# Preparing the token columns of a channel loop in two halves, placed behind the casts of the states

## The chip, the cores and the metric

The kernel runs on one core of one Trainium2 chip. The metric is the device time of one execution in microseconds (us), as the median of several runs. Before the change it is 2973.82 us, the median of 3 runs that lie between 2972.2 and 2982.99 us.

## The reference, cut to what matters

The program is the forward pass and all gradients of a gated layer. One branch is attention with 32 heads over 2048 tokens of width 576. The other is a diagonal state-space layer: each of 576 channels has 128 complex states and is convolved with a kernel K built from them. A sigmoid gate mixes the two.

```python
P = jnp.exp(logdA[:, :, None] * l[None, None, :])        # 576 x 128 x 2048
K = jnp.einsum("dn,dnl,dn->dl", Cc, P, dB).real
y = irfft(rfft(u, 2L) * rfft(K, 2L))[:L] + u * Dskip     # causal convolution
g = sigmoid((x * gate_w).sum(-1, keepdims=True))
out = g * attention(x) + (1 - g) * y
```

(The second half of this fence is condensed.) The output and the gradients of x, the weights, the state-space parameters and the gate are wanted.

## The kernel before, in words

The program runs in stages: projections, then the long attention stage (forward and backward), then a **channel loop** for the state-space branch, then a final stage that makes the weight gradients. The change touches the channel loop only. On the clock of the profile the loop fills roughly 2200 to 2768 us.

The loop handles the 576 channels in 18 blocks of 32 (`CB = 32`, `NBLK = 18`); two blocks make a pair of 64 channels (`XB = 2 * CB`). Time is cut into 16 chunks of 128 tokens (`NB = 16`, `NS = 15` chunk borders). The helpers, with their lines:

- `load_rx` (L879 to L884) loads, for a pair, the token columns of the input (xr_d) and of the incoming gradient (gyr_d) into `RXn`. There is one buffer of it.
- `prep_rx` (L886 to L891) turns `RXn` into `RX`, with three instructions on ScalarE (ACT): a reordering copy (L889), and two products with a column of token numbers (L890, L891). `RX` has two buffers; a buffer holds a pair. `m_fin` (L933) later adds two more columns per channel.
- `turn_e` (L946) transposes a half block of the powers E on TensorE (PE) and copies the result out on ACT (`E1e`, L957).
- `uv` (L968) multiplies `E1e` by the columns of `RX` on PE and copies the product out on ACT (`UV`, L982).
- `scan` (L984) is the recurrence over the 15 chunk borders. It runs on VectorE (DVE): 14 steps of three dependent instructions (L995, L998, L999) that make `HG`, the states.
- `casts` (L1001) makes bfloat16 copies of the states on ACT: `hR` and `gR` (L1006) and `CK` (L1008).
- `rw1`, `rw2` (L1010 to L1021) make the weights `Rw` on DVE from `HG`.
- `t0`, `ybp` (L1038, L1047) accumulate the outputs in PSUM on PE from `RX`, `T0w` and `Rw`; ACT copies them out (`yd`, L1059).
- `pairs1`, `pairs2` (L1077, L1084) are products of `UV` with `hR` and `gR` on DVE (`pq`, L1065 and L1093), summed on PE.
- `m_part` (L902), `m_skw` (L920), `m_sum` (L928), `k0` (L1023) serve the block that comes later: matmuls on PE, copies on ACT (`mst` L912, `wk` L1027, `K0c` L1035), and a trip through memory.

Iteration i of the loop (L1134) works on several blocks at once: block i (scan, casts, outputs, products), block i+1 (`uv`, second half of `turn_e`, `k0`), block i+2 (`turn_e` first half, `m_sum`, `m_fin`) and block i+3 (loads, `m_part`). In the source, `sb` is i+2. The loop also has a first round with i = -1, which has no current block.

The order of the work on PE, ACT, DVE and GpSimd (POOL) is written out by hand: L873 switches the scheduler off for these four engines, so each runs its instructions in the order in which the loop calls them. The queue of the transfers (SP) isn't in that list; its order is worked out when the program is built. Each of the engines works through its own list in order and waits at the first instruction whose input or buffer isn't there.

So the place where the loop calls `prep_rx` decides what stands behind it on ACT. Before the change it is called every second iteration, when i+2 is even, for a whole pair, ahead of `scan` and `casts`. On ACT, which has no part in the scan, it therefore stands directly before the casts `hR` and `gR` of the current block.

Of the kernel before, what the change touches and what calls it, by code (L numbers as in the profile page):

```python
# [11 lines left out]
BF = mybir.dt.bfloat16  # L12
# [5 lines left out]
P = 128  # L18


def build(tc, aps, dbg_aps=None, stages=("s1", "attn", "post", "s4", "final")):
# [7 lines left out]
    def mm(out, lhsT, rhs, start=True, stop=True, **kw):  # L29
        return nc.tensor.matmul(out, lhsT=lhsT, rhs=rhs, start=start, stop=stop, **kw)  # L30
# [31 lines left out]
    with ExitStack() as gctx:  # L62
# [38 lines left out]
        CB = 32  # L101
# [327 lines left out]
        if "attn" in stages:  # L429
# [5 lines left out]
            with ExitStack() as ctx:  # L435
# [266 lines left out]
                for G in range(NTOT + OFF + 24):  # L702
# [4 lines left out]
                    if G < NTOT:  # L707
                        u, s = divmod(G, NST)
                        g, b = units[u]
# [11 lines left out]
                    if r1:  # L721
                        g, b, i, j0 = r1
# [14 lines left out]
                    elif 0 <= m_ < NTOT // 8:  # L737
                        u_, kq = divmod(m_, NQ)
                        g, b = units[u_]
# [12 lines left out]
                        else:  # L752
                            p = 2 * kq + (slot == 4)
# [5 lines left out]
                    if r2:  # L759
                        g, b, s2 = r2  # L760
# [16 lines left out]
                    if G % 8 in (0, 3, 4, 7) and G >= 3:  # L777
                        i_ = (G - 3) // 8 * 4 + {3: 0, 4: 1, 7: 2, 0: 3}[G % 8]
                        u_, i_ = divmod(i_, NT)
                        if 0 <= u_ < NU:  # L780
                            g, b = units[u_]
# [13 lines left out]
                    for (kind, g, b, i, j, ps) in rows:  # L795
# [9 lines left out]
                        else:  # L805
# [6 lines left out]
                            if U["dsn", i] == nj:  # L812
                                p = i // 2
# [14 lines left out]
        if "s4" in stages:  # L828
            XB = 2 * CB
# [10 lines left out]
            with ExitStack() as ctx:  # L840
                pc = ctx.enter_context(tc.tile_pool(name="s4l", bufs=1))
                pw = ctx.enter_context(tc.tile_pool(name="s4lw", bufs=1))
# [31 lines left out]
                NCOL = 64  # L874
                CU0, CV0, CU1, CV1, CDK = 0, NB, 2 * NB, 2 * NB + NS, 2 * NB + 2 * NS
                RXs, BK = {}, {}
                ydx = {}

                def load_rx(xb):  # L879
                    d0 = xb * XB  # L880
                    RXn = pw.tile([P, 2 * NB, XB], BF, tag="RXn", bufs=1, name="RXn")
                    nc.sync.dma_start(RXn[:, 0:NB, :], xr_d[:, :, d0:d0 + XB])
                    nc.sync.dma_start(RXn[:, NB:2 * NB, :], gyr_d[:, :, d0:d0 + XB])
                    RXs[xb] = [RXn, None]  # L884

                def prep_rx(xb):  # L886
                    RXn = RXs[xb][0].rearrange("p k c -> p c k")
                    RX = RXs[xb][1] = pw.tile([P, XB, NCOL], BF, tag="RX", bufs=2, name="RX")
                    nc.scalar.copy(RX[:, :, 0:2 * NB], RXn)  # L889
                    nc.scalar.mul(RX[:, :, CU1:CU1 + NS], RXn[:, :, CU0:CU0 + NS], l1col)  # L890
                    nc.scalar.mul(RX[:, :, CV1:CV1 + NS], RXn[:, :, CV0:CV0 + NS], l0col)  # L891

                xss = {}

                def m_load(b):
                    xs = xss[b] = pw.tile([P, NSUB, SUB, CB], BF, tag="xs", bufs=2, name="xs")
                    src = bass.AP(tensor=xb_d.tensor, offset=xb_d[b:b + 1, 0:1, 0:1].offset,
                                  ap=[[XR * SUB * CB, NB], [SUB * CB, NSUB], [1, NSUB * SUB * CB]])
                    nc.sync.dma_start(xs.rearrange("p e t c -> p (e t c)"), src)
                    nc.sync.dma_start(gyp2[b % 2][:, 0:SUB, :].rearrange("p t c -> p (t c)"), gyb_d[b])  # L900
# [14 lines left out]
                def dkp(b):  # L915
                    return misc2[(b + 1) % 2][:, 12 * CB:13 * CB]
# [3 lines left out]
                def m_skw(b):  # L920
                    skw = skws[b] = pw.tile([P, CB // 8, P], F32, tag="skw", name="skw")
                    for v in range(CB // 8):
                        dd = b * CB + v * 8
                        src = bass.AP(tensor=Md_d.tensor, offset=Md_d[dd:dd + 1, 0:1, SUB - 1:SUB].offset,
                                      ap=[[2 * SUB * MW, 8], [MW - 1, SUB], [1, P]])
                        nc.sync.dma_start(skw[:, v, :], src)
# [6 lines left out]
                def m_fin(b):  # L933
                    RX = RXs[b // 2][1]
                    o = (b % 2) * CB
                    pk = dkp(b)
                    nc.scalar.copy(RX[:, o:o + CB, CDK], pk)
                    nc.scalar.mul(RX[:, o:o + CB, CDK + 1], pk, l0col)
                    nc.scalar.copy(dDs_row[:, b * CB:(b + 1) * CB], pk[0:1, :])

                def blk(b):
                    if b not in BK:
                        B_ = BK[b] = dict(E={}, En={})
                    return BK[b]
# [14 lines left out]
                def load_par(b):  # L959
                    par = blk(b)["par"] = pw.tile([P, 12, CB], F32, tag="par", bufs=2, name="par")  # L960
                    nc.sync.dma_start(par, par_d[:, 0:12, b * CB:(b + 1) * CB])

                def load_en(b, h):
                    dG = b * CB + h * GS
                    En = blk(b)["En"][h] = pw.tile([P, GS, 2, P], BF, tag="E1n", bufs=6, name="E1n")
                    nc.sync.dma_start(En, E_d[:, dG:dG + GS])

                def uv(b, h):  # L968
                    B_ = blk(b)
                    if h == 0:  # L970
                        B_["UV"] = pw.tile([P, 2, NCOL, CB], BF, tag="UV", bufs=2, name="UV")
                    UV = B_["UV"]
                    E_ = B_["E"].pop(h)
                    RX = RXs[b // 2][1]
                    off = (b % 2) * CB + h * GS
                    for q in range(2):
                        for ri in range(2):
                            pr = pps.tile([P, NCOL, 8], F32, tag="bk", bufs=4, name="uvp")
                            for c_ in range(8):
                                mm(pr[:, :, c_], lhsT=E_[:, q * 8 + c_, ri, :], rhs=RX[:, off + q * 8 + c_, :])  # L980
                            c0 = h * GS + q * 8
                            nc.scalar.mul(UV[:, ri, :, c0:c0 + 8], pr, -1.0 if ri == 0 else 1.0)  # L982
# [40 lines left out]
                def k0(b):  # L1023

                    B_ = blk(b)
                    wk = pw.tile([P, 2, CB], BF, tag="wk", bufs=2, name="wk")
                    nc.scalar.copy(wk, B_["par"][:, 10:12, :])  # L1027
                    kps = misc2[b % 2][:, 13 * CB:14 * CB]
                    mm(kps, lhsT=ident_bf[0:1, :], rhs=dsk_row[:, b * CB:(b + 1) * CB], start=True, stop=False)
                    for ch in range(CB):  # L1030
                        for ri in range(2):
                            mm(kps[:, ch:ch + 1], lhsT=B_["En"][ch // GS][:, ch % GS, ri, :], rhs=wk[:, ri, ch:ch + 1],
                               start=False, stop=(ch == CB - 1 and ri == 1))
                    K0c = pw.tile([P, CB], BF, tag="K0c", bufs=2, name="K0c")
                    nc.scalar.copy(K0c, kps)  # L1035
                    nc.sync.dma_start(Kp_d[b, P:2 * P, :], K0c)
# [97 lines left out]
                for i in range(-1, NBLK):  # L1134
                    cur = i >= 0
                    nx = i + 1 < NBLK
                    mb = i + 3 if i + 3 < NBLK else None
                    sb = i + 2 if i + 2 < NBLK else None
                    if sb is not None:
                        m_skw(sb)  # L1140
                    if sb is not None:
                        load_par(sb)
                    if mb is not None:
                        m_load(mb)
                    if sb is not None and sb % 2 == 0:
                        load_rx(sb // 2)
                    if nx and cur:
                        k0(i + 1)
                    if nx:
                        uv(i + 1, 0)  # L1150
                        turn_e(i + 1, 1, 0, 4)
                    if sb is not None and sb % 2 == 0:
                        prep_rx(sb // 2)
                    if cur:
                        scan(i, 0, 15)
                        casts(i)
                        rw1(i)
                        rw2(i)
                        t0(i, 0)
                        t0(i, 1)  # L1160
                    if nx:
                        uv(i + 1, 1)
                    if cur:
                        if nx:
                            t0_load(i + 1)
                        ybp(i, 0)
                        ybp(i, 1)
                        pairs1(i)
                    if cur and mb is not None:
                        load_en(mb, 0)  # L1170
                        load_en(mb, 1)
                    if sb is not None:
                        turn_e(sb, 0, 0, 4)
                        m_sum(sb)
                        m_fin(sb)
                    if cur:
                        pairs2(i)
                        sums(i)
                    if mb is not None:
                        m_part(mb, 0)  # L1180
                        m_part(mb, 1)
                    if cur:
                        BK.pop(i)
# [256 lines left out]
```

## Time and profile before

| | |
|---|---|
| time, median of 3 | 2973.82 us |
| span of the profiled execution | 2976.5 us |
| PE, DVE, ACT, POOL busy over the span | 83%, 79%, 80%, 54% |
| channel loop, 2262 to 2768 us: DVE, PE, ACT busy | 434.85, 386.21, 341.98 us of 506 |
| DMA engines busy in the same stretch, mean | 69% |
| reordering copy L889, 9 times, median | 3820 ns |
| products L890 and L891, 9 times each, medians | 2039 and 2104 ns |

How to read it: the shares over the whole span mix stages with different limits. The table's lower half is for the channel loop. DVE is the busiest engine there, and still not always busy; the question in this loop is what each engine waits for, and in which iterations. The views used are the timeline of each engine (a row is a run of like instructions with its start, its time from first start to last end, the count, and in brackets the idle time just before it with what ended it), the sums of waits, and the busy time by stretches.

### The profile page before, as it was taken

Reading aid. Unit: us, or ns where it says so; the run is one execution under the profiler, and the core shown is the slowest. Engines: PE = TensorE matmul, PEld = TensorE weight load, DVE = VectorE, ACT = ScalarE, POOL = GpSimd, SP = SyncE. Lnnn points to the kernel's source line nnn. Section 1 sums busy time; section 2 is a strip of 40 time slices with the busy share of each in tenths; the row PEclk is TensorE's granted clock in tenths of the full one; section 3 lists DMA queues with packets and bytes.
Section 4 is the critical chain, followed back from the end, with each engine's and each line's share of the span. In section 5 each row is a group of like instructions: output and inputs, shape, how many; then the busy total and the mean of one; then the engine's idle time right before and its main releaser. Section 6 shows DMA issues by size and latency. Waiting matters only on the chain.

```text
span 2976.5 us, 69573 instructions
## 1 busy us (share of the span) xinstructions
PE 2468.2 (83%) x27132; PEld 1186.9 (40%) x27132; DVE 2359.4 (79%) x4147; ACT 2373.2 (80%) x2765; POOL 1605.9 (54%) x2653
## 2 busy tenths in 40 slices
PE   4768988998988888889898889898847887876779
PEld 2432333332333233233333233333226777776457
DVE  4435998997998889799899889989937888889634
ACT  2449999999999999899999999999736777675111
POOL 1038888888887788778888878878010000000010
PEclk8877999998999999899999999999968888887889
DMA  8855999989989989998988998998788877872886
GB/s 224 160 152 107 159 155 169 163 158 165 171 147 165 167 155 167 160 157 155 168 165 154 164 161 153 166 165 153 130 196 217 209 201 208 206 194 66 244 211 132
DMA packets 1293343, 499.99 MB, mean 168 GB/s; under 512 B 1187774, under 2 KB 1263136, under 8 KB 1283796
## 3 DMA queue, kind: packets, MB, share of 16 engines
q1 hardware_dynamic: 1264500, 434.91, 77.2%
q0 software_dynamic: 20624, 53.26, 7.3%
q10 hardware_dynamic: 7888, 7.38, 0.8%
q8 instruction: 212, 3.47, 0.5%
q14 instruction: 119, 0.97, 0.1%
HBM read 144.48 MB, written 99.69 MB: 82 GB/s over the span
## 4 chain that ended last, share of the span: by engine, by line
ACT 34%; DVE 23%; PE 21%; DMA 8%; issue 7%; POOL 4%; SPq 3%; ACTq 0%; DVEq 0%; POOLq 0%
ACT eb L804 20%; ACT PT L799 13%; PE ps_P L30 7%; DVE ds L809 7%; DVE tz L995 3%; DVE HG L999 2%; DVE tz L998 2%; PE accV L30 2%; DMA gT<-gb 2%; PE turn_p L558 2%; PE ps_dx L30 2%; DVE pq L1065 2%; PE ps_dwq L30 1%; POOL et L358 1%; PE accK L30 1%
## 5 line engine op out<-in xcount | busy, mean ns | idle before, releaser
L809 DVE TENSOR_TENSOR ds<-ps_P,PT 128x512 bf16<-128x512 f32 x2048 | 1312.0, 683 | 123.0 <-PE ps_P L30 83.8
L804 ACT ACTIVATE eb<-ps_P 128x1024 bf16<-128x1024 f32 x1024 | 1098.6, 1073 | 71.9 <-PE ps_P L30 70.7
L799 ACT ACTIVATE PT<-ps_P 128x1024 bf16<-128x1024 f32 x1024 | 1101.8, 1078 | 3.7 <-PE ps_P L30 2.5
L30 PE MATMUL ps_P<-dOaT,VaT_g 32*128 32x512 bf16 x2048 | 581.4, 390 | 32.8 <-DVE ds L809 18.3
L358 POOL TENSOR_TENSOR et<-eG,eT 128x448 f32<-128x448 f32 x576 | 542.0, 961 | 10.7
L30 PE MATMUL ps_P<-QaT_g,KaT_g 32*128 32x512 bf16 x2048 | 416.3, 398 | 143.9 <-ACT PT L799 128.5
L30 PE MATMUL ps_P<-KaT_g,QaT_g 32*128 32x512 bf16 x2048 | 408.5, 391 | 2.2 <-ACT eb L804 1.6
L30 PEld LDWEIGHTS <-KaT_g 32*128 32x128 bf16 x2048 | 148.2, 92 | 477.4 <-issue 462.0
L358 POOL TENSOR_TENSOR Eo<-et,et 128x448 bf16<-128x448 f32 x288 | 327.0, 1135 | 20.8
L1101 POOL TENSOR_TENSOR SS<-m 128x96 f32<-128x96 f32 x18 | 7.9, 441 | 556.9 <-ACT m L1099 556.9
L30 PEld LDWEIGHTS <-QaT_g 32*128 32x128 bf16 x2048 | 116.1, 91 | 286.4 <-issue 264.7
L30 PE MATMUL accO<-PT,Vtok_g 128*32 128x512 bf16 x2048 | 214.4, 405 | 0.0
L30 PE MATMUL accV<-eb,dOa 128*32 128x512 bf16 x2048 | 185.3, 395 | 27.6 <-ACT eb L804 27.4
L30 PE MATMUL accK<-dsT,Qtok_g 128*32 128x256 bf16 x4096 | 166.2, 285 | 4.5 <-DMA dsT<-ds 2.8
L558 PE MATMUL turn_p<-ident_bf,ds 128*128 128x128 bf16 x1664 | 137.3, 227 | 29.9 <-DVE gb L630 28.8
L30 PE MATMUL accQ<-ds,Ktok_g 128*32 128x512 bf16 x2048 | 159.2, 388 | 3.2 <-DVE gb L612 2.6
L957 ACT COPY E1e<-etp 128x1024 bf16<-128x1024 bf16 x144 | 135.9, 1044 | 20.0 <-PE etp L956 14.6
L563 DVE COPY dsT<-turn_p 128x1024 bf16<-128x1024 bf16 (+1 forms) x224 | 144.2, 644 | 4.9 <-PE turn_p L558 4.9
L30 PEld LDWEIGHTS <-Vtok_g 128*32 128x32 bf16 x2048 | 53.8, 93 | 225.4 <-issue 224.6
L30 PE MATMUL yp<-Rw,E1n 128*128 128x30 bf16 x1152 | 67.8, 232 | 83.5 <-DVE Rw L1020 69.0
L30 PEld LDWEIGHTS <-E1n 128*128 128x128 bf16 x2304 | 96.5, 108 | 101.0 <-issue 100.5
L558 PEld LDWEIGHTS <-ds 128*128 128x128 bf16 x1664 | 100.5, 101 | 78.6 <-issue 78.6
(247 smaller groups left out, 3704.2 us busy)
## 6 DMA issues: line engine op xcount, KB each, us to landing
E_d<-Eo POOLq DMA_DIRECT2D x144, 256.0 KB, 3.8
E1n<-E_d SPq DMA_DIRECT2D x36, 1024.0 KB
xs<-xb_d SPq DMA_DIRECT2D x18, 1024.0 KB
T0w<-Kp_d SPq DMA_DIRECT2D x18, 1024.0 KB
Md_d<-mst SPq DMA_DIRECT2D x36, 288.0 KB
dsT<-ds SPq DMA_TRANSPOSE x512
dqkv_d<-dtk POOLq DMA_DIRECT2D x96, 72.0 KB, 4.4
QKV_d<-stg SPq DMA_DIRECT2D x12, 504.0 KB
```

The costliest lines, as they stand in the source:

```text
L30: return nc.tensor.matmul(out, lhsT=lhsT, rhs=rhs, start=start, stop=stop, **kw)
L358: nc.gpsimd.tensor_tensor(out, a, b, op=op)
L558: nc.tensor.transpose(pt_[:, x, qb, :], t_[:, qb * P:(qb + 1) * P], ident_bf)
L563: nc.vector.tensor_copy(o_(), pt_[:, x:x + n])
L799: nc.scalar.activation(U["PT"][i, j // 2], ps, ACT.Exp)
L804: nc.scalar.activation(e, ps, ACT.Exp)
L809: nc.vector.tensor_tensor(U["ds"][i][:, j, :], ps, U["PT"][i, j // 2][:, j % 2, :], op=A.mult)
L957: nc.scalar.copy(E_[:, 4 * q:4 * q + 4], pt_)
L995: nc.vector.tensor_tensor(tz, HG[:, :, k - 1, :].unsqueeze(1).to_broadcast([P, 2, 4, CB]), ZZ, op=A.mult)
L998: nc.vector.tensor_tensor(t0v, t0v, UVk[:, :, :, k, :], op=A.add)
L999: nc.vector.tensor_tensor(HG[:, :, k, :].rearrange("p (r s) c -> p r s c", s=2), t0v, t1v[:, ::-1], op=A.add)
L1065: nc.vector.tensor_tensor(o.rearrange("p a b n c -> p a b (n c)"), a_.rearrange("p b n c -> p b (n c)").unsqueeze(1).to_broadcast([P, 2, 2 ...
```

## The change

`prep_rx` now takes a block number instead of a pair number. It writes the half of `RX` that belongs to this block (32 of the 64 channels), with the same three instructions on half as many elements. The buffer is allocated with the first half. In the loop it is called in every iteration that has a block i+2, and its place is later: behind the casts, the weights and `t0` of the current block, and behind the second half of `uv`, so that on ACT it stands between the four `UV` copies and the two `yd` copies. Ahead of the loop, `prep_rx(0)` now prepares block 0 alone; block 1 follows in the round i = -1.

```diff
-                def prep_rx(xb):
-                    RXn = RXs[xb][0].rearrange("p k c -> p c k")
-                    RX = RXs[xb][1] = pw.tile([P, XB, NCOL], BF, tag="RX", bufs=2, name="RX")
+                def prep_rx(b):
+
+                    c0 = b % 2 * CB
+                    if c0 == 0:
+                        RXs[b // 2][1] = pw.tile([P, XB, NCOL], BF, tag="RX", bufs=2, name="RX")
+                    RXn = RXs[b // 2][0].rearrange("p k c -> p c k")[:, c0:c0 + CB]
+                    RX = RXs[b // 2][1][:, c0:c0 + CB]
                     nc.scalar.copy(RX[:, :, 0:2 * NB], RXn)
                     nc.scalar.mul(RX[:, :, CU1:CU1 + NS], RXn[:, :, CU0:CU0 + NS], l1col)
                     nc.scalar.mul(RX[:, :, CV1:CV1 + NS], RXn[:, :, CV0:CV0 + NS], l0col)
@@
                         turn_e(i + 1, 1, 0, 4)
-                    if sb is not None and sb % 2 == 0:
-                        prep_rx(sb // 2)
                     if cur:
                         scan(i, 0, 15)
                         casts(i)
@@
                     if nx:
                         uv(i + 1, 1)
+                    if sb is not None:
+                        prep_rx(sb)
                     if cur:
                         if nx:
                             t0_load(i + 1)
```

The order of the instructions on PE, DVE and POOL stays as it was. On ACT only the preparation moves and is cut in two. In the queue of transfers the second load of a pair (gyr_d) moves behind the `Md_d` stores of an odd iteration, the first (xr_d) behind the `par` load of that iteration, and some of the small loads change places with their neighbours (`skw` now ahead of the `K0c` store in every second iteration, `par` ahead of `gyp`). Lines from L886 on are up to four higher in the changed kernel.

## The prediction

> **What bounds the kernel now.** I read the chain that ended last first: most of it is attention, which the change doesn't touch, so I went to the channel loop alone. The busy time by stretches of two of its iterations (columns: length, then busy time and count of PE, weight loads, DVE, ACT, POOL, then clock, DMA share, GB/s) shows DVE at 50.61 of 58 us, PE 46.34, ACT 41.70, DMA at 0.81:
>
> ```profile
> 2371.00:2429.00 58.00, 46.34 (x779) 43.73 (x777) 50.61 (x105) 41.70 (x62) 1.82 (x4) 0.85 0.81 205
> ```
>
> Next, the timeline of DVE, at the products `pq`, once per iteration (0 to 3):
>
> ```profile
> 2270.78 2.23 DVE L1065 TENSOR_TENSOR pq<-UV,hR 128x1920 bf16<-128x1920 bf16 x2 [9.31 <-ACT hR L1006]
> ...
> 2297.81 2.23 DVE L1065 TENSOR_TENSOR pq<-UV,hR 128x1920 bf16<-128x1920 bf16 x2
> ...
> 2328.86 2.23 DVE L1065 TENSOR_TENSOR pq<-UV,hR 128x1920 bf16<-128x1920 bf16 x2 [4.21 <-ACT hR L1006]
> ...
> 2355.93 2.23 DVE L1065 TENSOR_TENSOR pq<-UV,hR 128x1920 bf16<-128x1920 bf16 x2
> ```
>
> From one `pq` to the next it is 27.03, 31.05, 27.07 us. An odd iteration has no wait: DVE runs without a gap, so 27.0 us is its own work. An even one is 4 us longer, and a wait for the cast `hR` stands in it. That wait occurs in 8 iterations, 38.6 us in all (the rows on tile `UV`): 9.31 in iteration 0, about 4.2 in the seven others (2, 4, ... 14). Who is late is seen on ACT, iteration 4 (even), then 5 (odd):
>
> ```profile
> 2374.68 3.76 ACT L957 COPY E1e<-etp 128x1024 bf16<-128x1024 bf16 x4 [0.26 <-PE etp L956]
> 2378.30 3.84 ACT L889 COPY RX<-RXn 128x2048 bf16<-128x2048 bf16 x1
> 2382.00 2.04 ACT L890 ACTIVATE RX<-RXn,l1col 128x960 bf16<-128x960 bf16 x1
> 2383.89 2.10 ACT L891 ACTIVATE RX<-RXn,l0col 128x960 bf16<-128x960 bf16 x1
> 2385.86 1.01 ACT L1006 CAST hR<-HG 128x960 bf16<-128x960 f32 x1
> ...
> 2407.30 0.99 ACT L1006 CAST hR<-HG 128x960 bf16<-128x960 f32 x1 [0.38 <-DVE HG L999]
> 2408.19 0.99 ACT L1006 CAST gR<-HG 128x960 bf16<-128x960 f32 x1
> 2409.09 0.29 ACT L1008 COPY CK<-UV 128x128 bf16<-128x128 bf16 x1
> 2409.29 2.04 ACT L982 ACTIVATE UV<-uvp 128x512 bf16<-128x512 f32 x4
> 2415.78 0.58 ACT L1059 CAST yd<-yp 128x512 bf16<-128x512 f32 x1 [4.45 <-PE yp L30]
> 2417.51 0.58 ACT L1059 CAST yd<-yp 128x512 bf16<-128x512 f32 x1 [1.14 <-PE yp L30]
> 2419.68 3.76 ACT L957 COPY E1e<-etp 128x1024 bf16<-128x1024 bf16 x4 [1.59 <-PE etp L956]
> ```
>
> In the even iteration the preparation holds ACT from 2378.30 to 2385.86, and `hR` goes only then. In the odd one ACT waits for DVE, and later stands idle 4.45 us before `yd`, which needs matmuls on `Rw`. Last, PE: it too waits for `Rw`, even in iteration 4.
>
> ```profile
> 2381.75 0.21 PE L30 MATMUL yp<-Rw,E1n 128*128 128x30 bf16 x1 [1.91 <-DVE Rw L1020]
> 2382.82 3.56 PE L30 MATMUL yp<-Rw,E1n 128*128 128x30 bf16 x63 [0.85 <-DVE Rw L1021]
> ```
>
> So DVE sets the pace, and even iterations carry one foreign wait.
>
> **What the Trainium skill says.** "ScalarE: Activation LUTs", section "What ACT_TABLE_LOAD costs", prices an ACTIVATE at a fixed part plus 0.833 ns per element: 186 ns fixed, some 93 more with a column operand, neighbours overlapping by about 93. The `E1e` copies agree: the pitch is (3.76-1.04)/3 = 0.905 us for 1024 elements, near 0.95 from the page. The reordering copy doesn't: 3.70 us of pitch for 2048 elements is 1.8 ns each. I scale its trace duration. "SBUF — State Buffer", section "SBUF: two separate sides", says PE and ACT have SBUF ports of their own and never wait for the others. The trace agrees for DVE: `wa` takes 2.16 us in the even iteration 2 beside the preparation and 2.16 in the odd 3. "TensorE: Matmul & The Clock Gate", section "Part 1: The HAM clock gate", has the PE clock fall to half after an idle window of about 3.4 us. After 5.04 us of idle time for `Rw` in iteration 1 the granted clock was 0.50 until about 2302.7. It was also 0.5 from 2313.2 to 2316.2 in mid-work, so I keep the throttled durations in PE's sum.
>
> **The change, part by part.**
>
> *Removed before `hR`:* 7.56 us of ACT (2385.86-2378.30). Without it `hR` starts when `E1e` ends and HG is done. In iteration 2 that is 2320.28 (start of L889), end 2321.3; DVE is ready for `pq` at 2328.86-4.21 = 2324.65. So 3.3 us are to spare, the whole wait goes, and the iteration falls to 27.03: 31.05-27.03 = 4.0 us, seven times = 28.1.
>
> *Iteration 0:* `hR` waited behind a preparation that itself waited for the gyr_d load until 2262.28. Now `hR` starts when `E1e` ends, 2261.7, and DVE gets it at 2262.65, not 2270.78: 8.1 us. (DVE is ready at 2261.47, so 1.2 of the 9.31 stay.) The preparation reaches its load some 4 us later than it did, so that wait ends too.
>
> *Added, each iteration, behind `UV`:* half of 7.56, 3.78 us, plus the fixed parts of three more instructions per pair. From the pitches of 512 elements (0.487) and 1024 (0.905) the fixed part is 0.07; from the page 0.09 to 0.19. That makes 0.2 to 0.5 us per pair, so 3.9 to 4.05 per half; I take 3.9. Behind it on ACT stand `yd`, then `E1e` of block i+2, and behind those PE's `bk` banks. In the odd iteration UV ends at 2411.33 and `yd` is due at 2415.78: 4.45 of room, 0.4 to 0.55 left, cost nothing, hidden by PE's wait for `Rw`. In an even iteration without the old preparation, from `E1e`'s end: hR, gR, CK, UV take 3.9 (2378.3 to 2382.2), the half ends at 2386.1, `yd` one could go at about 2384.6 and goes 1.5 late, `yd` two ends at 2387.2. The next `E1e` needs PE: 63 matmuls to 2386.4, the 15 sums 1.8, a first group 0.5, 2388.7. So ACT has 1.5 left, and the delay of `yd` is absorbed.
>
> *Ahead of the loop and i = -1:* ACT gives 3.6 us in the prologue, where it then idles 2.60 for a PE sum fed by a transfer; no gain. In i = -1 it gets 3.9 more before `E1e`, but then stands idle 1.22 and 6.49 us, until a gyp load lands and its matmuls run: no cost.
>
> *PE and DMA at the faster pace:* from iteration 1's `Rw` to iteration 2's, a 26.9 us round, PE is idle 0.86, 0.76 and 1.80 us: 23.5 of work, throttled parts included. DMA was busy 0.81 of 58 us per pair; over 54.1 that is 0.87. The moved loads stay early: by the queue's new order `gyp` goes right after `rw1`, some 11 us before its matmuls, and the later gyr_d load still leaves about half an iteration.
>
> *Sum.* `pq` of iteration 0 at 2262.65, then 17 rounds of 27.03: 2722.2. Before it was 2758.04 in the last. The gain is 35.9 (8.1 + 28.1, less rounding), and the final stage moves up by it: 2973.8-35.9 = 2938 us.
>
> **The rivals.**
>
> *PE or the transfers take over* at some 28 us a round. For it: PE has 3.4 idle in 26.9 and its clock varies; DMA near 0.9. Against: no wait for DMA among the sums of waits of 2400 to 2650 us on PE, ACT or DVE, and PE waits for DVE each round. Then 17x28 = 476 in place of 487.3 (2270.78 to 2758.04), with 8.1 from iteration 0: 19 less, 2954.
>
> *The wait only changes its name:* the half delays `yd`, this `E1e`, `mst` and `k0`, and each round averages what it did, 29. Against: the 0.4 and 1.5 us of room. Only iteration 0 gains, 2966, or nothing, 2974.
>
> *Slower:* the half falls whole onto the path each iteration, since a load that now comes late, or `yd`, holds everything: 27.03+3.95 = 30.98, 17 times 526.7, 39.4 more, less 8.1: 3005. Against: it needs all the room above to be gone.
>
> **How the numbers follow.** Forecast 0.80; PE or DMA 0.12; name changed 0.04; slower 0.04. 0.5% is 15 us, so faster means below 2959: 0.80 plus most of the second, 0.91; same 0.05, slower 0.04. The range 2929 to 2957 leaves out the last two and little else; its low end is the forecast less the 1.2 us left in iteration 0, 1.9 for rounds of 26.9 (the last ones of the loop take 26.92), 1.6 if the base is the fastest run before (2972.2), and some 4 for a spread of runs that was 11 us before.
>
> **What would show it.** Right: no `pq` wait for `hR` from iteration 1 on, `pq` every 27.0 us throughout, `L893` half copies near 1.95 us behind `UV`, and an idle time before the odd `yd` of about half a microsecond in place of 4.45. Wrong: a wait on DVE for `UV` or `hR`, `Rw` matmuls on PE no longer waiting for DVE, or any engine waiting for `skw`, `gyp` or `T0w`.

## The result, and the profile after

The changed kernel takes 2938.95 us, the median of 4 runs between 2934.51 and 2944.41; before it was 2973.01, the median of 4 as well. The ratio is 0.988, with a 95% interval of 0.985 to 0.991. The forecast was 2938.

Two rounds of the loop, from the `pq` of iteration 4 to that of iteration 6, in the busy time by stretches of the changed kernel (length, then busy time and count of PE, weight loads, DVE, ACT and POOL, then clock, DMA share, GB/s):

```profile
2366.40:2420.28 53.88, 44.80 (x778) 42.42 (x778) 50.50 (x105) 43.26 (x65) 2.08 (x4) 0.88 0.88 230
```

The same work now fills 53.88 us in place of 58. DVE does 50.50 of it, as before (50.61), so what went is idle time. DMA stands at 0.88 in these two rounds, where 0.87 had been worked out; over the 14 rounds from iteration 1 to 15 it is 0.82, and was 0.77 before. The timeline of DVE of the changed kernel, at the products `pq` of iterations 0 to 3:

```profile
2258.65 2.23 DVE L1069 TENSOR_TENSOR pq<-UV,hR 128x1920 bf16<-128x1920 bf16 x2 [1.68 <-ACT hR L1010]
...
2285.54 2.23 DVE L1069 TENSOR_TENSOR pq<-UV,hR 128x1920 bf16<-128x1920 bf16 x2
...
2312.56 2.23 DVE L1069 TENSOR_TENSOR pq<-UV,hR 128x1920 bf16<-128x1920 bf16 x2
...
2339.49 2.23 DVE L1069 TENSOR_TENSOR pq<-UV,hR 128x1920 bf16<-128x1920 bf16 x2
```

The rounds are 26.89, 27.02 and 26.93 us, and all 17 lie between 26.89 and 27.06. The bracket with the wait for `hR` is left in iteration 0 alone, with 1.68 in place of 9.31 us. The timeline of ACT, iteration 2:

```profile
2304.42 3.76 ACT L961 COPY E1e<-etp 128x1024 bf16<-128x1024 bf16 x4 [0.26 <-PE etp L960]
2308.04 1.02 ACT L1010 CAST hR<-HG 128x960 bf16<-128x960 f32 x1
2308.93 1.02 ACT L1010 CAST gR<-HG 128x960 bf16<-128x960 f32 x1
2309.83 0.33 ACT L1012 COPY CK<-UV 128x128 bf16<-128x128 bf16 x1
2310.03 2.09 ACT L986 ACTIVATE UV<-uvp 128x512 bf16<-128x512 f32 x4
2311.94 2.05 ACT L893 COPY RX<-RXn 128x1024 bf16<-128x1024 bf16 x1
2313.82 1.26 ACT L894 ACTIVATE RX<-RXn,l1col 128x480 bf16<-128x480 bf16 x1
2314.91 1.22 ACT L895 ACTIVATE RX<-RXn,l0col 128x480 bf16<-128x480 bf16 x1
2315.98 1.11 ACT L1063 CAST yd<-yp 128x512 bf16<-128x512 f32 x2
2318.56 1.01 ACT L961 COPY E1e<-etp 128x1024 bf16<-128x1024 bf16 x1 [1.47 <-PE etp L960]
```

`hR` starts as `E1e` ends and is done at 2309.06, 3.5 us before DVE's `pq` at 2312.56. Over iterations 1 to 15 it is 3.0 to 4.5 us early. The half takes 4.04 us (2311.94 to 2315.98), `yd` follows at once, and 1.47 us of idle time is left before the next `E1e` (0.2 to 1.5 in iterations 1 to 15). On PE, `Rw` of DVE is still the last to come:

```profile
2311.44 0.21 PE L30 MATMUL yp<-Rw,E1n 128*128 128x30 bf16 x1 [1.74 <-DVE Rw L1024]
2312.51 3.56 PE L30 MATMUL yp<-Rw,E1n 128*128 128x30 bf16 x63 [0.86 <-DVE Rw L1025]
```

**How the loop is measured below.** From run to run the stages that the change doesn't touch move by some microseconds: the last `eb` of attention, whose code is the same in all kernels here, starts anywhere from 2169.3 to 2183.0 us in the profiles of this study, and what follows the last `pq` takes 216 to 223. I therefore also compare a stretch that begins after attention: from the first `mst` copy of block 1 (the third `mst` of the loop, 2229.45 before, 2225.42 after) to the last `pq` (2758.04 and 2716.80). It took 528.59 us before and 491.38 after: 37.2 less. To the first `pq` it is 41.33 and 33.23, 8.1 less; from there to the last, 487.26 and 458.15, 29.1 less. The two profiles differ by 40.3 us in all: the stretch began 4.0 earlier in the second, it was 37.2 shorter, and what follows it took 0.9 longer. Each stretch below comes from the one profile of its kernel; only the changed kernel has two.

### The profile page after: what moved, and what is told of

Read it like the earlier page. It is cut to its first block, busy times and chain, and to the rows that moved or that the text cites. A ratio compares the mean times of both kernels' runs of the same rounds, so it can differ in the third digit from the quotient of the medians.

```text
span 2936.2 us, 69578 instructions
## 1 busy us (share of the span) xinstructions
PE 2460.4 (84%) x27132; PEld 1182.8 (40%) x27132; DVE 2357.5 (80%) x4147; ACT 2375.9 (81%) x2792; POOL 1606.4 (55%) x2653
## 4 chain that ended last, share of the span: by engine, by line
ACT 34%; DVE 24%; PE 21%; DMA 8%; issue 7%; POOL 4%; SPq 3%; ACTq 0%; DVEq 0%; POOLq 0%
ACT eb L804 20%; ACT PT L799 13%; PE ps_P L30 7%; DVE ds L809 7%; DVE tz L999 4%; DVE tz L1002 3%; DVE HG L1003 2%; PE accV L30 2%; PE turn_p L558 2%; PE ps_dx L30 2%; DMA gT<-gb 2%; PE ps_dwq L30 2%; PE accK L30 2%; DVE pq L1069 1%; POOL et L358 1%
```

## The experiments

The question was which part of the edit brings this: the place (`hR` no longer behind the preparation), or the size (half a pair in each iteration), and what sets the pace now.

**Cut in two, but not moved.** The changed kernel with the call back ahead of the scan:

```diff
                         turn_e(i + 1, 1, 0, 4)
+                    if sb is not None:
+                        prep_rx(sb)
                     if cur:
                         scan(i, 0, 15)
...
                         uv(i + 1, 1)
-                    if sb is not None:
-                        prep_rx(sb)
```

> The changed kernel with the halves put back ahead of the scan and the casts: cut in two, but not moved. Theory (the place matters: hR must not stand behind the preparation): the half takes 4.04 us of ACT, and in the changed kernel hR ends about 3.5 us before DVE wants it, so a wait of about 0.5 us for hR comes back in every round of DVE: rounds of 27.5 in place of 26.95, some 2947 us; iteration 0 loses about 4 us more, so 2951. Rival (the size matters: an even load on ACT is all that was needed): no wait for hR, rounds of 26.95, 2939 us. Second rival (a half in front of hR costs its whole length): rounds of 31, over 3000 us.

Measured: 2955.3 us (2940.9 to 2958.44), ratio 0.992 (0.989 to 0.994); the stretch from `mst` to the last `pq` is 499.14 us. The interval of the ratio overlaps with the changed kernel's, and of the 20.5 us between the two profiles only 7.8 lie in the stretch; the rest lies in stages that the edit doesn't touch. So the stretch has to decide. The timeline of DVE of this kernel, iterations 4 to 6:

```profile
2380.24 2.23 DVE L1069 TENSOR_TENSOR pq<-UV,hR 128x1920 bf16<-128x1920 bf16 x2 [0.29 <-ACT hR L1010]
...
2407.40 2.23 DVE L1069 TENSOR_TENSOR pq<-UV,hR 128x1920 bf16<-128x1920 bf16 x2 [0.31 <-ACT hR L1010]
...
2434.64 2.23 DVE L1069 TENSOR_TENSOR pq<-UV,hR 128x1920 bf16<-128x1920 bf16 x2 [0.42 <-ACT hR L1010]
```

The wait is back, but small: 0.2 to 0.55 us in 11 of the rounds. The mean of the 17 rounds is 27.13, 0.18 above the changed kernel's 26.95. So a half in front of `hR`, 3.95 us long here, costs far less than its length: most of it falls into the time by which `hR` had been early. That was the theory's sign, at a third of its size. The larger loss, 4.6 us (37.86 in place of 33.23 from `mst` to the first `pq`), lies ahead of it: the half of round -1 stands before the second `UV` of block 0 here, and the first `HG` comes 14.3 us after `mst` in place of 9.2. The theory had the 4 us, but in a wait of iteration 0, and there was none beyond 1.26.

**Moved, but not cut in two.** The kernel before with its call for a pair at the new place:

```diff
-                    if sb is not None and sb % 2 == 0:
-                        prep_rx(sb // 2)
                     if cur:
                         scan(i, 0, 15)
...
                         uv(i + 1, 1)
+                    if sb is not None and sb % 2 == 0:
+                        prep_rx(sb // 2)
```

> The kernel before with the preparation of a whole pair moved to the new place, every second iteration: moved, but not cut in two. Theory (the place matters): no wait for hR, DVE rounds of 27.0 in even and odd iterations; the 7.5 us push yd and the E1e copies behind it back by about 2.5 us in even rounds, of which PE has about 1.5 to spare, and the odd round takes up the rest; 2939 to 2944 us. Rival (the halving is needed): yd and E1e late by more than the rest of the round has, so DVE waits again in even rounds by 2 to 4 us, 2955 to 2974 us.

Measured: 2941.77 us, ratio 0.988 (0.986 to 0.989); stretch 492.75 us, rounds of 26.9 to 27.06 but for one of 27.89, the first. The timeline of ACT of this kernel, iteration 2 and part of 3:

```profile
2315.61 4.19 ACT L889 COPY RX<-RXn 128x2048 bf16<-128x2048 bf16 x1
2319.53 2.23 ACT L890 ACTIVATE RX<-RXn,l1col 128x960 bf16<-128x960 bf16 x1
2321.48 2.15 ACT L891 ACTIVATE RX<-RXn,l0col 128x960 bf16<-128x960 bf16 x1
2323.38 1.21 ACT L1059 CAST yd<-yp 128x512 bf16<-128x512 f32 x2
2324.32 3.92 ACT L957 COPY E1e<-etp 128x1024 bf16<-128x1024 bf16 x4
...
2340.00 1.03 ACT L1006 CAST hR<-HG 128x960 bf16<-128x960 f32 x1
...
2346.06 0.58 ACT L1059 CAST yd<-yp 128x512 bf16<-128x512 f32 x1 [1.98 <-PE yp L30]
```

7.8 us stand before `yd` (2315.61 to 2323.38), and `E1e` has no idle time left before it; still the next `hR` ends at 2341.03, and DVE takes its `pq` at 2344.24 without a wait. The delay is used up within ACT's and PE's spare time of the two rounds. The place alone brings 35.8 of the 37.2 us. The halving is not needed for it.

**Only iteration 0 moved.** The kernel before, with the preparation of iteration 0 at the new place and the seven others left:

```diff
-                    if sb is not None and sb % 2 == 0:
+                    if sb is not None and sb % 2 == 0 and i != 0:
                         prep_rx(sb // 2)
...
                         uv(i + 1, 1)
+                    if i == 0:
+                        prep_rx(sb // 2)
```

> The kernel before with only the preparation of iteration 0 moved to the new place (whole), the seven others left where they were. Theory: the wait for hR in iteration 0 falls from 9.31 to about 1.7 us and the seven waits of 4.2 us stay; 8 us less than before, 2965 us. Rival (the loop start is held by transfers, and the wait comes back as another one in round 1): the time from the first HG copy to the product of iteration 2 as before, 2973 us.

Measured: 2969.7 us, ratio 0.997 (0.996 to 0.998); stretch 522.33, 6.3 less than before, where 8 had been expected. The timeline of DVE, iterations 0 to 2:

```profile
2266.80 2.23 DVE L1065 TENSOR_TENSOR pq<-UV,hR 128x1920 bf16<-128x1920 bf16 x2 [1.41 <-ACT hR L1006]
2294.67 2.23 DVE L1065 TENSOR_TENSOR pq<-UV,hR 128x1920 bf16<-128x1920 bf16 x2 [1.07 <-ACT hR L1006]
2326.29 2.23 DVE L1065 TENSOR_TENSOR pq<-UV,hR 128x1920 bf16<-128x1920 bf16 x2 [4.79 <-ACT hR L1006]
```

The first wait falls from 9.31 to 1.41 us, as the theory had it. A part comes back: with the whole pair at once, round 1 waits 1.07 us, and the wait of iteration 2 grows by 0.6. The whole pair moved in every iteration has the same 1.07 in round 1. At the start of the loop, then, and only there, the halves are worth about a microsecond.

**The half twice.** The changed kernel, each half prepared a second time behind itself, which writes the same values again (`again=True` keeps the buffer that is there):

```diff
                     if sb is not None:
                         prep_rx(sb)
+                        prep_rx(sb, again=True)
```

> The changed kernel with every half prepared twice in the loop, so 4.04 us more of ACT in each iteration at the new place. Theory (DVE sets the pace, ACT has room): E1e would start about 2.5 to 3 us later, PE's idle time before Rw (1.3 to 1.7 us a round) shrinks to nothing, hR still ends before DVE wants it; rounds of 27.0 to 27.5, 2939 to 2948 us. Rival (the half just fitted, and what stands behind it sets the pace): most of the 4 us shows in each round, rounds of 29.5 to 31, 2980 to 3008 us.

Measured: 2956.07 us, ratio 0.993 (0.991 to 0.996); stretch 509.42, loop from first to last `pq` 473.95, rounds of 27.02 to 28.36, mean 27.88. The sums of waits of this kernel, 2300 to 2650 us (total, times, longest):

```profile
PE psM L30 <- ACT E1e L961: 34.7, 12, 3.2
...
PE misc L30 <- ACT m L1103: 18.5, 13, 1.4
...
DVE pq L1069 <- ACT hR L1010: 13.9, 13, 1.4
```

Of 4 us more in each round 0.93 show: the rest was spare. Once `E1e` is late, PE waits for it with `psM`, which takes its PSUM banks from the same four as the transposes that `E1e` has not yet copied out; the copies behind that go late, and at last `hR`. Both theories missed: the room is less than I had put it, and much more than the rival's nothing.

**What sets the pace now.** The changed kernel with less work for DVE. The first leaves out the two pD products, the second those and pC; the sums on PE read another product in their place, so PE's work stays, and the gradients made from these sums get other values.

```diff
-                    for ri in range(2):
-                        nc.vector.tensor_tensor(pD[:, ri, :, 0:NS - 1, :], ...)
-                    psum(b, 2, [pD], NS - 1)
+                    psum(b, 2, [pC], NS - 1)
```

> The changed kernel without the two pD products of pairs2 (the gradient sums that use them get other values; the sum on PE keeps its 14 matmuls and reads pC). This takes some 1.1 us of DVE from each of 18 blocks. Theory (DVE sets the pace of the changed loop): rounds of 25.9 us, 18 to 20 us less than the changed kernel, 2920 us. Rival (PE or ACT has taken over the pace, and DVE only waits less visibly): rounds of 26.8 to 27, a wait on DVE of about 1 us, 2937 us.

> The changed kernel without the pC product and the two pD products (their sums on PE read pB again, so PE does the same work; gradient sums get other values). DVE loses some 2.2 us a block: 24.8 us of its own per round. Theory (PE is next, with 1.3 to 1.7 us idle before Rw in the changed kernel, which fall to 0): rounds of 25.3 to 25.6, DVE waiting 0.5 to 0.8 us, no idle time on PE before Rw, 2911 to 2916 us. Rival (ACT's list is next): rounds of 26 or more with waits for hR. Rival (DVE still sets the pace): rounds of 24.8, 2902 us.

Measured: 2924.17 us and rounds of 25.82 to 26.00 without pD; 2911.64 us and rounds of 24.75 to 24.94, but for a first one of 25.68, without pC and pD. The timeline of DVE of the second, iterations 5 and 6:

```profile
2390.78 2.23 DVE L1069 TENSOR_TENSOR pq<-UV,hR 128x1920 bf16<-128x1920 bf16 x2
...
2415.57 2.23 DVE L1069 TENSOR_TENSOR pq<-UV,hR 128x1920 bf16<-128x1920 bf16 x2
```

No wait even now. Each microsecond taken from DVE comes off the round, two in a row. PE's waits for the first `Rw` instruction, 2300 to 2650 us, in the changed kernel and then in the second of these:

```profile
PE yp L30 <- DVE Rw L1024: 26.4, 13, 3.0
...
PE yp L30 <- DVE Rw L1024: 5.2, 9, 0.9
```

So DVE sets the pace of the changed loop, with at least 2 us between it and PE. My expectation that PE would stop the second at 25.3 fell. I had read PE's spare time as the 1.3 to 1.7 us of the first iterations; over these 13 rounds of the changed kernel it is 2.0 on average (26.4 us in all), and 26.95 less 2.0 is already 24.9. PE's own work was also 0.4 us a round shorter in this run (below). The time, 2911.64, lies in the range named for the theory that fell; the rounds, 24.9, are those of the rival in which DVE still sets the pace.

**One DVE instruction moved to ACT.** Since DVE is the bound and ACT has room, a small step that computes the same: the copy of the first state goes to ACT, behind the `UV` copies.

```diff
+                def hg0(b):
+                    ...
+                    nc.scalar.copy(B_["HG"][:, :, 0, :].rearrange("p (r s) c -> p r s c", s=2), UVk[:, :, :, 0, :])
...
                         uv(i + 1, 1)
+                        hg0(i + 1)
```

> The changed kernel with the copy of the first state (one DVE cast of 0.22 us a block) moved to ACT, behind the four UV copies and ahead of the half preparation. Theory (DVE sets the pace, ACT has some 1 to 2 us of room): rounds of 26.7, 4 us less than the changed kernel over 17 rounds, at the limit of what the times can tell. Rival (the first step of the scan now waits for ACT): rounds of 26.95 or more with a wait for HG from ACT.

> The changed kernel once more, unaltered, beside the next three on one chip: rounds of DVE of 26.9 to 27.0 us, the loop from the first pq to the last in 458 us, a ratio to before of 0.985 to 0.990. If it comes out elsewhere, stages outside the loop move by that much from run to run.

Measured on one chip: 2937.87 us with it (2930.78 to 2946.18, ratio to before 0.987, 0.984 to 0.990), 2947.23 us for the changed kernel once more (2940.82 to 2950.85, ratio 0.989, 0.986 to 0.992). The intervals overlap, so the times alone don't settle it. The profiles do for the loop: rounds of 26.65 to 26.83 against 26.90 to 27.07, 454.00 against 458.38 us from the first `pq` to the last, no wait for `hR` or `HG`. That is 4.4 us, the expected 0.25 a round. The changed kernel's own stretch repeats to 0.02 us (491.36 and 491.38), while its profiled spans are 2943.4 and 2936.2.

## Why the prediction was right

**How near.** That the median lies within 1 us of the forecast is partly luck. Its four runs spread over 10 us, and when the changed kernel was timed once more it gained 30.8 us in the medians, in place of 34.1. In the pair of profiles the loop gained 37.2, where 35.9 was forecast. What follows is about the parts of that sum.

**The pace.** That DVE's 27.0 us of its own set the round, and that even rounds carried one foreign wait, held: rounds of 26.89 to 27.06 after, and experiments with less DVE work follow DVE one to one.

**Removed before `hR`.** Seven times 4.0 us, 28.1, was forecast; 29.1 came off, since the odd rounds too are 0.1 shorter (26.95 on average, not 27.03). The 3.3 us to spare between `hR` and DVE in iteration 2 measured 3.5, and 3.0 to 4.5 up to iteration 15. The experiment with the halves at the old place agrees with it from the other side: a half of 3.95 us in front of `hR` brings back waits of at most 0.55 from iteration 1 on. The 0.3 us by which the sum, 35.9, misses its two parts isn't rounding alone: the last two rounds before had been 26.92 and 26.91, not 27.03.

**Iteration 0.** 8.1 forecast, 8.1 measured from `mst` to the first `pq`. The wait that stays is 1.68, not 1.2; in the repeated run it was 0.29, so it varies.

**The half behind `UV`.** 3.9 was taken out of 3.9 to 4.05; it is 4.04, and its reordering copy takes 2.04 (median), not 1.95. By the medians two halves, 4.05 each, take 0.6 us more than the whole before, 7.52, but three more instructions per pair are not all of that. At the same place they cost 0.4: two halves of 3.95 against 7.52 for the whole at the old one, two of 4.05 against 7.73 at the new. So the 0.07 each, read off the pitches of plain copies, was too small. The upper end, an estimate of 0.5 from the price of an ACTIVATE with a column operand in the Trainium skill, "ScalarE: Activation LUTs", section "What ACT_TABLE_LOAD costs", was nearer. The other 0.1 us per half comes with the place; why, no run here shows.

**Where a step was wrong, without harm.** For odd rounds I put the half into 4.45 us of idle time before `yd` and left "0.4 to 0.55". In the changed kernel there is no such idle time in any iteration that has a half: `yd` follows the half at once. As I read the traces, the 4.45 had been there because the even round before was stretched by DVE's wait, and ACT and PE had used it to run ahead: in the odd round before, `hR` waited 0.38 us for `HG`, and in iteration 2 of the changed kernel it starts 2.2 us after the last `HG` (2305.86 to 2308.04), behind `E1e`. No experiment tests this by itself. Without the stretched rounds, all rounds look like the one I worked out for even ones: `yd` late, then 1.5 us left before `E1e`. That figure came out at 1.47 in iteration 2, and at 0.2 to 1.5 in the others up to 15. So the sum was safe because of the second case, not the first.

A second slip did no harm either. To see whether DVE is slowed beside ACT, I read `wa` of iteration 2, but it ended (2320.32) just as the preparation began (2320.28). The instruction beside it is `wb`:

```profile
2320.23 2.15 DVE L1014 TENSOR_TENSOR wb<-HG,par 128x1920 f32<-128x1920 f32 x1
```

It takes 2.15 us in every iteration, so DVE is not slowed there.

**Transfers and PE.** DMA reads 0.80 to 0.88 in the pairs of rounds that begin in iterations 0 to 12, against the 0.87 worked out, and there is no wait for a load on PE or DVE between 2300 and 2650 us. PE's idle time before `Rw` is 1.47, 1.74 and 1.58 us in iterations 1 to 3, against the 1.80 read before, and 1.3 to 3.1 up to iteration 15. The rivals that give time back are ruled out by the rounds. The one in which the wait only changes its name needed more of ACT than there was: it shows with the half prepared twice, and there at 0.93 us a round.

**What the forecast didn't say.** It gave the whole effect to the place. That is nearly right, but cutting in two without moving brought 29.4 of the 37.2 us, and moving without cutting 35.8. The two parts of the edit are two ways to nearly the same gain, not two gains: moving leaves none of the preparation in front of `hR`, and cutting leaves 3.95 us, about as much as `hR` may be late.

## What to carry to other kernels

A wait in every second round is best read against the rounds that lack it: their length is the pace without the wait, and the gain is the difference of the two, not the busy time that was moved. Work on an engine off the path costs far less than its length where what stands behind it may be late, so before cutting or moving it, ask how late its successor may be; one of the two edits may do. And idle time seen in a round that follows a stretched one may not be room: here it was gone when the stretching was.

## What the runs showed of the hardware

PE's busy time for the same work moves from round to round; the change did not shorten it. The 14 rounds from the `pq` of iteration 1 to that of iteration 15, before and after:

```profile
2297.81:2704.21 406.40, 324.50 (x5434) 306.53 (x5434) 354.35 (x728) 292.38 (x427) 12.93 (x28) 0.85 0.77 199
...
2285.54:2662.97 377.43, 325.27 (x5434) 308.24 (x5434) 353.95 (x728) 298.30 (x450) 13.22 (x28) 0.87 0.82 216
```

The same 5434 matmuls took 324.50 us and 325.27. Two rounds alone can mislead: the two shown with the result have 44.80 us, those from iteration 2 to 4 have 47.73 for the same 778 matmuls. Without pC and pD the 14 rounds took 319.58 us, at a mean granted clock of 0.91.

One group shows what moves. In the changed kernel the 15 sums of `pairs1` took 1.02 us at 2369.75, where the granted clock was 1.00, and 1.78 at 2315.89, where it was 0.50. Before, they took 1.76 or 1.78 in every iteration from 0 to 15. A sum of PE durations read from one round is therefore not that of the next, and several rounds are needed. What sets the clock wasn't tested.
